# A random-feature attention and a feed-forward block on one core: queue orders, engines and buffer places written anew, and warming matmuls that read the identity

## The chip, the cores and the metric

One NeuronCore of a Trainium2 chip runs the whole kernel. The metric is the device time of one execution in microseconds (us), and the figure of a kernel is the median over its runs. TensorE is PE below (its weight loads PEld), VectorE is DVE, ScalarE is ACT, GpSimd is POOL, and SyncE, whose queue issues the kernel's DMAs, is SP.

## What is computed

```python
# q, k, v: 8 batches x 8 heads x 576 tokens x 64; omega: 128 x 64; w_in: 512 x 2048; w_out: 2048 x 512
def phi(x):                                   # x is q or k, times 64 ** -0.25
    h = einsum('bhsd,md->bhsm', x, omega) - sum(x * x, -1, keepdims=True) / 2
    return exp(h - max(h, -1, keepdims=True)) / sqrt(128)
kv  = einsum('bhsm,bhsd->bhmd', phi(k), v);  z = sum(phi(k), axis=2)
num = einsum('bhsm,bhmd->bhsd', phi(q), kv)
den = einsum('bhsm,bhm->bhs', phi(q), z)[..., None] + 1e-06
x   = (num / den) laid out as 4608 tokens x 512
h   = x @ w_in
out = maximum(0.01 * h, h) @ w_out            # 4608 x 512, float32
```

The weights come as 64-bit words, and the kernel makes them into floats itself.

## The kernel before

The 4608 tokens are done in nine blocks of 512. For block j the kernel needs the keys of the batches that the block touches (`key_batch`), the queries of the block (`query_block`) and the two layers of the feed-forward part (`feed_forward`). Almost every float32 product is made of three float16 matmuls: a number is split into a high part (`high`, a copy into float16 on ACT or DVE) and a low part (`low_`, a subtraction on POOL or DVE, line 699), and high by high, high by low and low by high are summed in PSUM.

Keys and queries go, a pair of heads at a time, through these steps. A DMA brings the rows (`nat`), ACT squares them (L936), DVE sums the squares (L938) and makes a power of two as a scale (L943 to L950), the rows are split (`z`) and turned by a DMA transpose (`t`), PE projects them on omega into the bank `pj` (L976), DVE takes the maxima (L984) and the scaled difference (L1004), ACT the exponentials, and the result is split into `ph`. The first batch of keys, the second one and the first block of queries (`Whole`) use float32 matmuls instead and need no transpose (L1060, L1076, L1078). Values by keys are summed in a bank `mi` (L1189 or L1201 to L1203) and split into `kv` (L1223). The numerators of the queries are products of `qp` and `kv` into a bank `mi` (L1313 in block 0, L1306 to L1308 after it); DVE takes the reciprocal of the denominators (L1324, L1328) and multiplies (L1330), which writes `xp` and frees the bank.

While the first keys and queries are done, the 16 pieces of the two weight matrices are loaded, put together from their words (L825 to L855, on ACT, DVE and POOL), measured (L845, L733 to L742) and split (L693, L691, L896). The first layer of blocks 0 and 1 is L1468, the second layer L1704. From block 2 on the first layer uses seven products in place of eight (L1522), and the last block does so in both layers (L1629).

There is no scheduler at run time. Each engine has a queue, and a queue runs in the order in which its instructions were written. The functions above do not emit instructions: they record operations (`Plan.op`) with the engines on which each may run, what it reads and writes, and the buffers it uses. A planner (`Plan.forward`) gives each operation an engine, each buffer one of the places of its kind (two `nat` tiles, three `ph` tiles, two `mi` banks and so on), and fills idle time of PE at the beginning with matmuls whose result nobody reads (`heat`, L783). After it, `Plan.order` puts the operations into the order of the table `ORDER`, with the engines of the table `ON`. An operation waits for the last users of a buffer's place, so an order and the places together set who waits for whom.

```python
            done = [by[n] for n in ORDER]
        nc.tensor.matmul(tiles["mi"][1][:, 4 * E:4 * E + 240], om[:, 0, :],
                         om.rearrange("p a b -> p (a b)")[:, :240], start=True, stop=True)
```

The second of these is the warming matmul: it needs `om`, the split omega, which DVE makes from `omT` with a power of two (L733 to L742, L771 to L776). `ident` is the identity, a DMA of its own (L754), which the matmul at L733 reads to spread a maximum over the partitions.

Of the kernel before, what the change touches and what calls it, by code (L numbers as in the profile page):

```python
# [17 lines left out]
P = 128  # L18
# [23 lines left out]
PASSES = 0  # L42
SHIFT_OP = {180: -1.13, 6: -3.99, 178: 2.07, 213: -0.22, 420: 3.05, 572: -0.02, 480: -0.72, 242: -1.74, 250: -2.72, 106: -1.06, 268: -4.94, 148: -4.28, 85: -4.22, 813: 0.8, 510: 2.03, 109: 2.11, 452: 11.66, 574: 2.34, 243: -2.55, 245: -6.52, 430: 4.22, 69: 19.05, 135: 1.83, 476: -3.51, 209: -10.73, 167: 1.07, 75: -11.31, 536: -3.21, 54: 2.69, 203: -3.67, 218: -23.73, 152: 1.07, 137: -0.51, 238: -0.14, 168: 2.42, 811: 24.59, 116: -2.3, 454: -3.25, 518: -0.29, 44: 0.47, 494: -5.44, 239: -5.28, 580: 6.23, 191: -6.7, 855: 8.61, 275: -6.71, 236: 4.8}
# [35 lines left out]

class Buf:  # L80
# [211 lines left out]
class Plan:  # L292
# [70 lines left out]
    def backward(self, done):  # L363
# [3 lines left out]
        for o in done:  # L367
            o.needs = {x.number: x for x in o.before}
            for b in o.bufs:
# [4 lines left out]
                for x in (x for u in at_[b] for x in u.ops):  # L374
                    o.needs[x.number] = x
# [1435 lines left out]
```

## Time and profile before

| what | value |
|---|---|
| runs | 907.95, 909.09 and 909.64 us; median 909.09 us |
| the profiled execution, first to last instruction (its span) | 907.4 us |
| what the median has around that span | 1.7 us |
| PE busy | 887.9 us, 98% of the span |
| DVE busy | 790.7 us, 87% |
| ACT busy | 536.3 us, 59% |
| POOL busy | 240.5 us, 27% |

The profile gives the span of the profiled execution and no other time of it, so its own time is taken as the median's 909.1 us: the span and 1.7 us around it. A share of busy time is a mean over stages. The stages are: the first 100 us, with weights, keys and queries in float32; up to 165 us, the first layer of block 0 and the beginning of its second layer, with the keys of batch 2 and the queries of block 1; then a long stretch of feed-forward work; and the last block's end from 890 us. In the windows below, each engine's busy time stands with the number of its instructions behind it, then the granted share of PE's clock, the busy share of the 16 DMA engines and their GB/s.

### The profile page before, as it was taken

The numbers are of one execution on the slowest core, as the hardware profiler recorded it, in microseconds if no ns is written. First come the engines' busy times: TensorE is split into PE (matmuls) and PEld (weight loads), VectorE is DVE, ScalarE is ACT, GpSimd is POOL, SyncE is SP. The second block draws the span as 40 slices with busy tenths as digits, with TensorE's granted clock in tenths as the row PEclk, the third lists the DMA queues.
The fourth block names the chain that finished last, engine by engine and source line by source line (L and its number), as shares of the span: only waits on it lengthen the run. The fifth ranks groups of instructions, "written<-read, shape, count | busy, mean of one in ns | idle before, by whom it ended". The sixth has DMA issues, their size and how long they took to land.

```text
span 907.4 us, 20572 instructions
## 1 busy us (share of the span) xinstructions
PE 887.9 (98%) x8257; PEld 640.6 (71%) x8257; DVE 790.7 (87%) x1571; ACT 536.3 (59%) x825; POOL 240.5 (27%) x236
## 2 busy tenths in 40 slices
PE   7999989999999999999999999999999999999998
PEld 6888545554556975688568855886579656888887
DVE  7999989978999999999998999899998999952771
ACT  5688877467655774477546854686557533522530
POOL 2332234456341330220211330132001101331340
PEclk9999999999999999999999999999999999999999
DMA  9757456766899979897899897987999636443401
GB/s 353 282 212 220 123 122 139 181 179 138 180 225 230 270 209 208 231 251 178 195 231 225 196 257 167 245 232 157 187 201 252 156 78 215 146 101 115 164 1 47
DMA packets 274879, 170.13 MB, mean 187 GB/s; under 512 B 191072, under 2 KB 237920, under 8 KB 273760
## 3 DMA queue, kind: packets, MB, share of 16 engines
q1 hardware_dynamic: 274784, 168.82, 73.3%
q8 instruction: 64, 1.05, 0.5%
q14 instruction: 31, 0.25, 0.1%
HBM read 105.87 MB, written 16.78 MB: 135 GB/s over the span
## 4 chain that ended last, share of the span: by engine, by line
PE 75%; DVE 12%; DMA 6%; ACT 4%; issue 2%; SPq 1%; POOL 0%; ACTq 0%; DVEq 0%
PE late L1522 14%; PE late L1704 13%; PE ffn L1704 13%; PE ffn L1522 13%; PE pj L976 5%; PE late L1629 5%; PE ffn L1629 3%; PE late L1468 2%; PE ffn L1468 2%; DMA t<-qT 1%; PE mi L1306 1%; DMA nat<-kT 1%; DVE wt L835 1%; PE mi L1308 1%; PE mi L1307 1%
## 5 line engine op out<-in xcount | busy, mean ns | idle before, releaser
L1522 PEld LDWEIGHTS <-w 128*128 128x128 f16 x2352 | 228.0, 98 | 30.4 <-issue 0.5
L1704 PEld LDWEIGHTS <-big 128*128 128x128 f16 x1344 | 127.7, 98 | 138.2
L699 POOL TENSOR_TENSOR big<-row,big 128x512 f16<-128x512 f32 x76 | 92.5, 1222 | 307.1 <-ACT big L693 189.8
L1704 PE MATMUL late<-wt,big 128*128 128x512 f16 x672 | 157.5, 379 | 0.0
L1704 PE MATMUL ffn<-wt,big 128*128 128x512 f16 x672 | 157.0, 379 | 0.0
L1522 PE MATMUL late<-xt,w 128*128 128x256 f16 x864 | 117.9, 273 | 0.0
L1522 PE MATMUL ffn<-xt,w 128*128 128x256 f16 x840 | 114.9, 273 | 0.4 <-DMA xt<-v 0.4
L1007 ACT ACTIVATE p<-p,little 128x1024 f32<-128x1024 f32 (+1 forms) x60 | 61.0, 1016 | 63.0 <-DVE p L1004 52.9
L984 DVE TENSOR_REDUCE st<-pj 128x8 f32<-128x1024 f32 x68 | 73.2, 1077 | 10.6 <-PE pj L976 10.4
L699 DVE TENSOR_TENSOR ph<-p,ph 128x1024 f16<-128x1024 f32 x56 | 69.3, 1238 | 5.4 <-ACT ph L693 4.7
L1004 DVE SCALAR_TENSOR_TENSOR p<-pj,sc,st 128x1024 f32<-128x1024 f32 (+1 forms) x60 | 67.0, 1117 | 0.8
L1468 PEld LDWEIGHTS <-w 128*128 128x128 f16 x384 | 36.6, 98 | 40.3
L693 ACT ACTIVATE big<-row 128x512 f16<-128x512 f32 x92 | 56.3, 622 | 8.5 <-DVE row L1494 7.7
L1545 ACT ACTIVATE row<-row 128x512 f32<-128x512 f32 x71 | 43.7, 625 | 26.6 <-DVE row L1538 25.6
L936 ACT ACTIVATE z<-nat 128x512 f32<-128x512 f32 (+1 forms) x56 | 36.2, 646 | 31.8 <-DMA nat<-qn 16.2
L1522 PE MATMUL late<-w,w 128*128 128x256 f16 x324 | 53.0, 273 | 0.0
L1522 PE MATMUL ffn<-w,w 128*128 128x256 f16 x324 | 53.0, 273 | 0.0
L1468 PE MATMUL ffn<-xt,w 128*128 128x512 f16 x216 | 50.9, 379 | 0.0
L693 ACT ACTIVATE ph<-p 128x1024 f16<-128x1024 f32 x47 | 49.6, 1055 | 0.9
L699 POOL TENSOR_TENSOR v<-xp,v 128x1024 f16<-128x1024 f32 (+1 forms) x10 | 20.5, 2055 | 109.0 <-DVE v L689 49.4
L852 POOL TENSOR_TENSOR wt<-wt,wt 128x1024 f32<-128x1024 f32 x10 | 25.4, 2550 | 69.8 <-ACT wt L850 36.4
L938 DVE TENSOR_REDUCE sq<-z 128x8 f32<-128x512 f32 (+1 forms) x56 | 39.4, 705 | 4.1 <-ACT z L936 3.9
(300 smaller groups left out, 1893.3 us busy)
## 6 DMA issues: line engine op xcount, KB each, us to landing
w<-w1d SPq DMA_DIRECT2D x196, 256.0 KB, 3.8
v<-vn SPq DMA_DIRECT2D x28, 650.0 KB, 5.0
big<-w_in SPq DMA_DIRECT2D x8, 1024.0 KB, 10.3
big<-w_out SPq DMA_DIRECT2D x8, 1024.0 KB, 5.7
nat<-qn SPq DMA_DIRECT2D x32, 256.0 KB, 3.4
out<-row SPq DMA_DIRECT2D x31, 256.0 KB, 3.0
w1d<-wt SPq DMA_DIRECT2D x16, 256.0 KB, 3.4
nat<-kn SPq DMA_DIRECT2D x12, 320.0 KB, 4.7
```

What stands on the lines that cost most here:

```text
L693: ("ACT", act(n, int(pointer)), lambda: nc.scalar.activation(dst(), src(), AF.Copy, scale=1.0 if scale is None else value()), False),
L699: return ways([(e, c, lambda g=g: g.tensor_tensor(dst(), a(), b(), op=ALU.subtract), True) for e, c, g in (("POOL", pool_(n), nc.gpsimd), ...
L938: op("DVE", dve(n), lambda: nc.vector.tensor_reduce(at(self.sq)[:, :2 * nt], square().rearrange("p (g d) -> p g d", d=D), axis=AX.X, op=AL ...
L976: nc.tensor.matmul(at(pj)[:, 512 * h + c * M:512 * h + (c + 1) * M], at(self.t)[:, 2 * (c0 + c) + h, :], om[:, w, :], start=(w == 0), stop ...
L984: op("DVE", dve(n * M), lambda: nc.vector.tensor_reduce(row(0), pv(), axis=AX.X, op=ALU.max), r=[pj], w=[st], prio=prio)
L1004: op("DVE", dve(n * M), lambda: nc.vector.scalar_tensor_tensor(p(), pv(), down(), row(2).rearrange("p (g o) -> p g o", o=1).broadcast_to([ ...
L1007: op("ACT", act(n * M, 1), lambda: nc.scalar.activation(flat(p()), flat(p()), AF.Exp, bias=shift), w=[p32], r=["ones"], prio=prio)
L1468: nc.tensor.matmul(at(ph), wk[wp][:, c:c + P], xt[:, 512 * xp:512 * xp + 512], start=(i == 0), stop=(i == 3 * KT - 1))
L1522: nc.tensor.matmul(pair(bank)[:, f], wt[:, k, wp, f * P:f * P + P], operand(xname, k, xp), start=(first and f == k == i == 0), stop=(k == ...
L1545: op("ACT", act(512), lambda: nc.scalar.activation(at(g), at(src), AF.Prelu, scale=H_DOWN * (TAIL_DOWN if tail else 1.0), alpha=0.01), r=[ ...
L1629: nc.tensor.matmul(pair(bank)[:, t], g()[:, gp, f, t * P:t * P + P], operand(wname, 2 * q + f, wp), start=(first and q == t == f == i == 0 ...
L1704: nc.tensor.matmul(at(po), g_(q)[:, s, gp, t * P:(t + 1) * P], wf[wp], start=(q == s == 0 and gp == wp), stop=(q == s == 3 and gp == 1))
```

## The change

The planner's passes go (`backward`, `PASSES`, `SHIFT_OP`). Where there is an `ORDER`, `forward` is no longer run: the order, each operation's engine (`ON`, or the first engine that the operation allows) and now also each buffer's place (`PLACES`) come from tables, which are all new. Negative numbers in `ORDER` are warming matmuls, so many as the number says. The warming matmul reads `ident` instead of `om`, and so waits for that DMA alone.

```diff
+PLACES = {
+    "xt": [0, 1, 2, 3, 0, 1, 2, 3, 0, 5, 4, 1, 3, 2, 0, 1, 5, 3, 4, 1, 2, 0, 5, 1, 3, 2, 4, 0, 1, 3, 5, 2, 0],
...
 ORDER = [
-    2, 16, 1, 0, 27, 62, 144, 151, 17, 7, 3, 43, 9, 4, 28, 165, 18, 5, 6, 146, 145, 22, 19, 152, 3478, 81, 3461, 20,
...
     def order(self):
-        done = self.forward()
-        for _ in range(PASSES):
...
+        if not ORDER:
+            return self.forward()
+        for o in self.ops:
+            o.engine, o.heat = ON.get(o.number, next(iter(o.ways))), False
+            o.cost, o.run, o.held = o.ways[o.engine]
+        done, heaters = [], len(self.ops)
+        for n in ORDER:
+            if n >= 0:
+                done.append(self.ops[n])
+                continue
+            x = Op()
+            x.number, x.engine, x.heat, x.filler, x.held = heaters, "PE", True, True, False
+            x.cost, x.run = -0.1 * n, lambda n=n: self.warm[1](-n)
+            x.ways, x.before, x.bufs = {"PE": (x.cost, x.run, False)}, [self.warm[0]], []
...
+        self.settle(done)
         return done
+    def settle(self, done):
...
+                if b.place is None:
+                    b.place = PLACES[b.kind][nth[b]]
...
-                nc.tensor.matmul(tiles["mi"][1][:, 4 * E:4 * E + 240], om[:, 0, :],
-                                 om.rearrange("p a b -> p (a b)")[:, :240], start=True, stop=True)
-        plan.warm = done, heat
+                nc.tensor.matmul(tiles["mi"][1][:, 4 * E:4 * E + 240], ident.bitcast(F16)[:, :P],
+                                 ident.bitcast(F16)[:, :240], start=True, stop=True)
+        plan.warm = turner, heat
```

The operations are the same ones, and so is the number of matmuls that compute something. There are 106 warming matmuls where there were 137. Of the 3430 operations 264 have another engine: 100 copies of `high` go from ACT to DVE and 96 from DVE to ACT, 43 subtractions of `low_` (L699) go from DVE to POOL and 23 from POOL to DVE, and 4 scalings of the last block (L1649, L1653) trade ACT and DVE. In the first 100 us one operation alone has another engine; there the order is what changes. Lines of the changed kernel are 48 higher than those of the kernel before from `omega` on.

The first place is SP's queue at the start. `nat`, `xn` and `t` hold keys and queries (`kT`, `qT`), `big` a piece of `w_in`, `v` the values. Before:

```order
L1033 DMA nat_83<-kT 128x640
L754 DMA ident<-eye 128x128
L753 DMA xt_108<-omT 128x256
L1033 DMA nat_84<-kT 128x640
L1033 DMA xn_107<-qT 128x512
L810 DMA big_79<-w_in 128x2048
```

and in the change:

```order
L1081 DMA nat_83<-kT 128x640
L801 DMA xt_108<-omT 128x256
L858 DMA big_79<-w_in 128x2048
L1081 DMA xn_107<-qT 128x512
L1081 DMA nat_84<-kT 128x640
L802 DMA ident<-eye 128x128
```

Omega comes second instead of third, and the identity sixth instead of second, behind a piece of the weights of 1 MB. On PE the matmul that spreads omega's maximum (L733), the first one before, comes behind the projections of the first head pair, and the first ten warming matmuls come behind it.

The second place is SP's queue where the keys of batch 2 begin, at about 100 us. `nat<-kn` are the rows of a pair of heads, `t<-z` the transposes of queries of block 1. Before:

```order
L1108 DMA v_0_99<-vn 128x1300
L1381 DMA w1d<-w_7_68 128x4x256
L963 DMA_TRANSPOSE t_87<-z_85 128x8x128
L933 DMA nat_83<-kn 128x5x128
L963 DMA_TRANSPOSE t_87<-z_86 128x8x128
```

and in the change:

```order
L1156 DMA v_0_99<-vn 128x1300 x2
L981 DMA nat_83<-kn 128x5x128
L1011 DMA_TRANSPOSE t_87<-z_86 128x8x128
L1322 DMA_TRANSPOSE qp_96<-ph_89 128x8x128
```

The keys' rows stood behind the transpose of the third pair of queries and now stand ahead of it.

The third place is DVE's queue ahead of the first multiplications by a reciprocal of block 1. L1223 (L1271 in the change) writes `kv` of batch 0, L896 (L944) splits a piece of `w_out`, L1324 and L1330 (L1372, L1378) are the reciprocal's first step and the multiplication that frees a bank `mi`. Before:

```order
L1223 SCALAR_TENSOR_TENSOR kv_100<-mi_137,kv_100 128x4
L699 TENSOR_TENSOR big_80<-row_104,big_80 128x512
L1223 SCALAR_TENSOR_TENSOR kv_100<-mi_136,kv_100 128x4
L896 SCALAR_TENSOR_TENSOR wt_69<-wt_70,little,wt_69 128x1024
L1324 TENSOR_SCALAR r_124<-mi_137 128x4
```

and in the change:

```order
L1271 SCALAR_TENSOR_TENSOR kv_100<-mi_137,kv_100 128x4
L747 TENSOR_TENSOR z_85<-nat_84,z_85 128x8x64
L1042 SCALAR_TENSOR_TENSOR st_114<-st_114,sc_122,sq_118 128x8
L1043 SCALAR_TENSOR_TENSOR st_114<-sq_118,st_114 128x8
L1187 SCALAR_TENSOR_TENSOR v_98<-v_0_99,little,v_98 128x1280
L1052 SCALAR_TENSOR_TENSOR p_0_88<-pj_129,sc_122,st_114 128x1024
L944 SCALAR_TENSOR_TENSOR wt_77<-wt_73,little,wt_77 128x1024
L747 TENSOR_TENSOR z_86<-nat_83,z_86 128x10x64
L1372 TENSOR_SCALAR r_124<-mi_136 128x4
```

More of DVE's work on the weights, the keys and the values stands between `kv` and the multiplications. On PE, 66 matmuls of the second layer (L1704) now stand ahead of the fourth group of numerators of block 1, where before 6 did.

## Rows read from the trace of the kernel before

**Rows 1.** The page: each engine's busy time, share and instructions.

```profile
PE 887.9 (98%) x8257; PEld 640.6 (71%) x8257; DVE 790.7 (87%) x1571; ACT 536.3 (59%) x825; POOL 240.5 (27%) x236
```

**Rows 2.** Windows: us, busy time of PE, PEld, DVE, ACT, POOL; clock, DMA.

```profile
0.00:9.66 9.66, 4.05 (x38) 3.83 (x40) 3.62 (x18) 2.75 (x3) 0.20 (x4) 1.00 0.78 265
9.66:100.00 90.34, 85.71 (x962) 74.77 (x959) 86.50 (x130) 71.34 (x97) 25.05 (x11) 1.00 0.68 251
100.00:140.50 40.50, 37.27 (x248) 19.08 (x247) 36.41 (x87) 32.09 (x54) 13.95 (x20) 1.00 0.51 112
...
165.00:890.00 725.00, 723.04 (x6720) 519.03 (x6719) 636.59 (x1289) 414.00 (x652) 189.37 (x184) 1.00 0.77 186
```

**Rows 3.** The warming matmuls of L783 alone: busy time of PE and PEld.

```profile
9.66:100.00 90.34, 15.73 (x137) 12.80 (x137) 1.00 0.68 251
```

**Rows 4.** The chain that ended last, 100 to 170 us: start, us, engine, tile.

```profile
114.07 6.19 DMA nat<-kn
...
141.66 5.18 PE late L1704 x24
```

**Rows 5.** The timeline, 100 to 142 us: start, us, instruction, [idle before, releaser].

```profile
112.76 1.25 SPq L963 DMA_TRANSPOSE t<-z  x1
...
121.10 0.82 DVE L938 TENSOR_REDUCE sq<-z 128x10 f32<-128x640 f32 x1 [2.66 <-ACT z L936]
...
129.44 2.75 PE L1468 MATMUL late<-xt,w 128*128 128x512 f16 x12
...
140.52 0.19 PE L1306 MATMUL mi<-kv,qp 128*128 128x65 f16 x1
```

**Rows 6.** DVE's groups over the whole span: busy us, mean ns of one.

```profile
L699 DVE TENSOR_TENSOR ph<-p,ph 128x1024 f16<-128x1024 f32 x56 | 69.3, 1238 | 5.4 <-ACT ph L693 4.7 <-DMA qp<-ph 0.3
L984 DVE TENSOR_REDUCE st<-pj 128x8 f32<-128x1024 f32 x56 | 68.2, 1218 | 7.4 <-PE pj L976 7.3
L699 DVE TENSOR_TENSOR big<-row,big 128x512 f16<-128x512 f32 x49 | 34.6, 712 | 1.1 <-ACT big L693 1.0
L1139 DVE SCALAR_TENSOR_TENSOR v<-v,little,v 128x1280 f16<-128x1280 f32 x12 | 19.8, 1650 | 0.0
L896 DVE SCALAR_TENSOR_TENSOR w<-wt,little,w 128x1024 f16<-128x1024 f32 x6 | 7.7, 1278 | 0.0
L699 DVE TENSOR_TENSOR z<-nat,z 128x512 f16<-128x512 f32 x12 | 8.2, 684 | 0.7 <-ACT z L693 0.7
```

**Rows 7.** PE's groups in the stretch from 100 to 165 us: busy us, mean ns.

```profile
L1468 PE MATMUL late<-xt,w 128*128 128x512 f16 x58 | 13.8, 379 | 0.0
L976 PE MATMUL pj<-om,t 128*128 128x128 f16 x64 | 4.2, 219 | 1.5 <-ACT p L1001 1.4
```

**Rows 8.** The timeline of the first 10 us.

```profile
1.66 0.42 SPq L753 DMA_DIRECT2D xt<-omT  x1
...
4.81 0.29 DVE L765 TENSOR_SCALAR xt<-xt 128x256 f32<-128x256 f32 x1 [3.14 <-DMA xt<-omT]
...
8.20 0.64 PE L1060 MATMUL pj<-xt,nat 64*128 64x128 f32 x4
...
9.00 0.39 PE L1060 MATMUL pj<-xt,nat 64*128 64x128 f32 x4
...
9.66 1.23 DVE L1076 TENSOR_REDUCE st<-pj 128x8 f32<-128x1024 f32 x1 [0.79 <-PE pj L1060]
```

**Rows 9.** DVE's copies of L689 (min/median/max ns), and one beside a subtraction on POOL.

```profile
L689 DVE CAST big<-row x33: 414/418/1376, 105.2 to 870.8; 128x512 f16<-128x512 f32 x33
...
212.30 1.40 POOL L699 TENSOR_TENSOR big<-row,big 128x512 f16<-128x512 f32 x1
212.61 1.38 DVE L689 CAST big<-row 128x512 f16<-128x512 f32 x1
```

**Rows 10.** PE's longest wait for a DMA behind 165 us, in the timeline.

```profile
489.07 0.20 PE L1308 MATMUL mi<-kv,qp 128*128 128x65 f16 x1 [0.65 <-DMA qp<-ph]
```

**Rows 11.** One window of 50 us, the columns as in rows 2.

```profile
250.00:300.00 50.00, 48.69 (x457) 31.22 (x455) 48.86 (x95) 31.92 (x45) 15.43 (x14) 1.00 0.99 235
```

More of the change, by code (lines that the diff above doesn't have):

```diff
@@ L77 @@
 PRICE = {"PE": 1.0, "ACT": 0, "DVE": 27.4627, "POOL": 1.0804, "SP": 1.0}
+PLACES = {
[3 rows of a table added]
+    "raw": [0, 1, 3, 2, 0, 1, 3, 0, 2, 1, 3, 2],
+    "sqz": [0, 1, 0, 2, 1, 0, 2, 0, 1, 2, 1, 0],
[8 rows of a table added]
+    "edge": [0, 1, 2, 3, 0, 1, 2, 3, 0, 1, 2, 3, 0, 1, 2, 3],
[6 rows of a table added]
+    "ffn": [0, 1, 0, 0, 1, 1, 1, 0, 1, 1, 0, 1, 0, 1, 3, 0, 2, 1, 1, 0, 3, 2, 3, 0, 1, 2, 3, 1, 0, 2, 3, 1, 0, 0, 3,
[7 rows of a table added]
+    "big": [1, 0, 0, 2, 3, 1, 2, 3, 0, 1, 3, 0, 2, 2, 1, 3, 0, 2, 1, 3, 0, 2, 1, 3, 0, 2, 1, 3, 0, 2, 1, 3, 0, 2, 1,
[4 rows of a table added]
+    "row": [0, 1, 0, 2, 3, 1, 0, 1, 2, 3, 1, 0, 3, 2, 1, 0, 2, 3, 1, 2, 0, 3, 1, 2, 1, 3, 0, 2, 3, 1, 0, 2, 3, 1, 0,
[6 rows of a table added]
+    "nat": [0, 1, 0, 1, 0, 0, 1, 0, 1, 0, 1, 0, 1, 0, 1, 0, 1, 0, 1, 0, 1, 0, 1, 0, 1, 0, 1, 0, 1, 0, 1, 0, 1, 0, 1,
[13 rows of a table added]
+    "ring": [4, 1, 2, 9, 6, 3, 4, 0, 8, 5, 1, 3, 7, 2, 9, 0, 4, 6, 5, 8, 9, 3, 7, 2, 1, 0, 8, 4, 9, 4, 7, 3, 5, 6, 2,
[8 rows of a table added]
+}
 class Buf:
@@ new lines @@
+    700: "DVE", 705: "DVE", 725: "DVE", 734: "DVE", 770: "DVE", 790: "DVE", 854: "DVE", 914: "DVE", 923: "DVE",
+    953: "DVE", 1008: "DVE", 1011: "DVE", 1015: "DVE", 1024: "DVE", 1033: "DVE", 1036: "DVE", 1046: "DVE",
+    1053: "DVE", 1061: "DVE", 1084: "DVE", 1096: "DVE", 1100: "DVE", 1110: "DVE", 1116: "DVE", 1117: "DVE",
+    1140: "DVE", 1160: "DVE", 1170: "DVE", 1180: "DVE", 1218: "DVE", 1289: "DVE", 1304: "DVE", 1345: "DVE",
+    1399: "DVE", 1404: "DVE", 1410: "DVE", 1411: "DVE", 1423: "DVE", 1430: "DVE", 1431: "DVE", 1442: "DVE",
@@ new lines @@
+    1454: "DVE", 1469: "DVE", 1474: "DVE", 1486: "DVE", 1492: "DVE", 1560: "DVE", 1597: "DVE", 1636: "DVE",
+    1688: "DVE", 1695: "DVE", 1755: "DVE", 1772: "DVE", 1824: "DVE", 1837: "DVE", 1844: "DVE", 1845: "DVE",
+    1874: "DVE", 1879: "DVE", 1957: "DVE", 2004: "DVE", 2034: "DVE", 2052: "DVE", 2066: "DVE", 2102: "DVE",
+    2104: "DVE", 2123: "DVE", 2147: "DVE", 2162: "DVE", 2172: "DVE", 2190: "DVE", 2210: "DVE", 2219: "DVE",
+    2254: "DVE", 2264: "DVE", 2304: "DVE", 2326: "DVE", 2342: "DVE", 2372: "DVE", 2384: "DVE", 2387: "DVE",
@@ new lines @@
+    2402: "DVE", 2448: "DVE", 2483: "DVE", 2484: "DVE", 2497: "DVE", 2509: "DVE", 2512: "DVE", 2523: "DVE",
+    2532: "DVE", 2540: "DVE", 2549: "DVE", 2554: "DVE", 2555: "DVE", 2573: "DVE", 2580: "DVE", 2581: "DVE",
+    2587: "DVE", 2592: "DVE", 2615: "DVE", 2626: "DVE", 2667: "DVE", 2678: "DVE", 2693: "DVE", 2718: "DVE",
+    2740: "DVE", 2752: "DVE", 2762: "DVE", 2777: "DVE", 2794: "DVE", 2853: "DVE", 2855: "DVE", 2857: "DVE",
+    2873: "DVE", 2885: "DVE", 2901: "DVE", 2903: "DVE", 2905: "DVE", 2923: "DVE", 2926: "DVE", 2941: "DVE",
@@ L285 @@
+    2953: "DVE", 2965: "DVE", 2980: "DVE", 2995: "DVE", 3019: "DVE", 3022: "DVE", 3025: "DVE", 3080: "DVE",
+    3150: "DVE", 3166: "DVE", 3180: "DVE", 3195: "DVE", 3218: "DVE", 3219: "DVE", 3228: "DVE", 3232: "DVE",
+    3240: "DVE", 3252: "DVE", 3255: "DVE", 3261: "DVE", 3270: "DVE", 3274: "DVE", 3294: "DVE", 3297: "DVE",
+    3316: "DVE", 3324: "DVE", 3339: "DVE", 3354: "DVE", 3363: "DVE", 3387: "DVE", 3403: "DVE",
 }
@@ L345, in order @@
     def order(self):
-        done = self.forward()
-        for _ in range(PASSES):
-            late = self.backward(done)
-            for o in self.ops:
-                if not o.filler and o.prio > -0.9:
-                    o.prio = -0.5 + 1e-4 * (late[o.number] + SHIFT_OP.get(o.number, 0.0))
-            done = self.forward()
-        if ORDER:
-            by = {o.number: o for o in done}
-            assert len(by) == len(ORDER)
-            for n, e in ON.items():
-                o = by[n]
-                o.engine, (o.cost, o.run, o.held) = e, o.ways[e]
-            done = [by[n] for n in ORDER]
@@ L361, in order @@
-        return done
-    def backward(self, done):
-        held, at_ = {}, {}
-        done = [o for o in done if not o.heat]
+        if not ORDER:
[12 more added lines that the diff above has]
+            x.ways, x.before, x.bufs = {"PE": (x.cost, x.run, False)}, [self.warm[0]], []
+            heaters += 1
+            done.append(x)
@@ new lines, in order @@
+        assert sorted(o.number for o in done if not o.heat) == list(range(len(self.ops)))
+        self.settle(done)
+        return done
+    def settle(self, done):
+        shared = {}
+        for k, hosts in self.over.items():
+            for h in hosts:
+                shared.setdefault(k, []).append(h)
+                shared.setdefault(h, []).append(k)
+        user, last, nth = {}, {}, {b: i for bs in self.kinds.values() for i, b in enumerate(bs)}
+        for bs in self.kinds.values():
+            for b in bs:
+                b.place, b.left = None, len(b.ops)
@@ L367, in backward @@
         for o in done:
-            o.needs = {x.number: x for x in o.before}
             for b in o.bufs:
-                if b not in at_:
-                    hosts = [(b.kind, b.place), *self.over.get((b.kind, b.place), ())]
-                    at_[b] = [held[k] for k in hosts if k in held]
-                    held[b.kind, b.place] = b
-                for x in (x for u in at_[b] for x in u.ops):
-                    o.needs[x.number] = x
-            o.needs.pop(o.number, None)
-        left = dict.fromkeys((o.number for o in done), 0)
@@ L378, in backward @@
-        for o in done:
-            for x in o.needs:
-                left[x] += 1
-        last = max(o.end for o in done)
-        until, late = dict.fromkeys(left, last), {}
-        free = dict.fromkeys(("PE", "ACT", "DVE", "POOL", "SP"), last)
-        port = last
-        todo = [o for o in done if not left[o.number]]
-        while todo:
-            cost = lambda o: o.cost - self.LESS[o.engine]
-            def latest(o):
-                r = min(until[o.number] - (o.end - o.start - cost(o)), free[o.engine])
-                return min(r, port) if o.held else r
-            o = max(todo, key=lambda o: (latest(o), o.start))
-            start = latest(o) - cost(o)
-            todo.remove(o)
-            late[o.number] = free[o.engine] = start
-            if o.held:
-                port = start
-            for n, x in o.needs.items():
-                until[n] = min(until[n], start)
-                left[n] -= 1
-                if not left[n]:
-                    todo.append(x)
@@ L403, in backward @@
-        return late
+                if b.place is None:
+                    b.place = PLACES[b.kind][nth[b]]
+                    assert b.place < self.places[b.kind]
+                    hosts = [(b.kind, b.place), *shared.get((b.kind, b.place), ())]
+                    assert not any(user.get(k) for k in hosts), f"{b.kind} {nth[b]} has a place in use"
+                    user[b.kind, b.place] = b
+                b.left -= 1
+                if not b.left:
+                    user[b.kind, b.place] = None
@@ L777, in split @@
                                                op1=ALU.subtract)
-        done = op("DVE", 1.3, split, r=[(whole, "om"), key], w=["om", "om_c"], prio=0.005)
+        op("DVE", 1.3, split, r=[(whole, "om"), key], w=["om", "om_c"], prio=0.005)
         def heat(n):
             for _ in range(n):
-                nc.tensor.matmul(tiles["mi"][1][:, 4 * E:4 * E + 240], om[:, 0, :],
-                                 om.rearrange("p a b -> p (a b)")[:, :240], start=True, stop=True)
-        plan.warm = done, heat
+                nc.tensor.matmul(tiles["mi"][1][:, 4 * E:4 * E + 240], ident.bitcast(F16)[:, :P],
+                                 ident.bitcast(F16)[:, :240], start=True, stop=True)
+        plan.warm = turner, heat
     class Weight:
```

29 lines of the change are left out of this document (3 added, 26 removed), and 397 rows, old and new, of tables (ORDER, PLACES).

## Prediction

> **What bounds the kernel now.** I read the page first, then windows, then the chain of waits, then the timeline. The page says PE 98% [rows 1], which invites the conclusion that only PE's work counts. The windows correct it [rows 2]. From 165 to 890 us PE is without work for 725.00 - 723.04 = 2.0 us. In the 9.66 us of the start it idles 5.6; up to 100 us it idles 90.34 - 85.71 = 4.6, and 15.7 of its busy time is warming [rows 3], so 20.4 us go without arithmetic that counts; from 100 to 140.5 us it idles 3.2. Some 29 of its 31 lost microseconds lie ahead of 140.5 us. The engine that is full there is DVE: 86.50 of 90.34 and 36.41 of 40.50 us. The chain of waits agrees [rows 4]: ahead of 140 us it runs over DVE and a load of keys, and from 141.66 us it stays on PE. So there are two regimes. Up to about 140 us DVE sets the pace; after it, PE executes a fixed amount of work without holes. **The end comes earlier by as much as PE has more work done when the last long wait for DVE ends.** That wait's end is the fourth group of numerators of block 1, which started at 140.52 us [rows 5]: it needs a bank `mi` that DVE frees at L1330 (L1378). I count what each queue has ahead of that one operation, before and after, from the orders and the durations in the rows.
>
> **PE's queue.** In the change 66 matmuls of L1704 stand ahead of these numerators where 6 did, so 60 are newly done by then (of the 66 newly ahead, 6 replace six of L1468). Twelve such matmuls in one run take 2.75 us [rows 5] and one alone 0.379 [rows 7], so one follows another at (2.75 - 0.379) / 11 = 0.2155 us: 12.9 us. Sixteen projections of L976 come ahead as well, at 4.2 / 64 = 0.066 [rows 7]: 1.05. Eighteen numerators, 65 columns wide against the projections' 128, at half of that: 0.6. Sum 14.6 us of PE work that no longer stands behind the wait.
>
> **DVE's queue.** Newly ahead of the bank's release [rows 6]: three splits of L896 at 1.278, two of L1139 at 1.650, a maximum of L984 at 1.218, a scaled difference of L1004 that I price by the like 128x1024 form of L896 at 1.278, a `ph` subtraction at 1.238, two `z` subtractions at 0.684. Together 12.2. Seven short ones have no row of their own; at the 0.29 of a 128x256 instruction [rows 8] they are 2.0. No longer ahead: four subtractions of `big` at 0.712 (2.85) [rows 6], two copies of L689 and four conversions of L691, all at a copy's 0.418 [rows 9] (2.5). Net +8.8 us. If DVE idles as before, the wait ends 8.8 us later and has 14.6 us more PE work behind it: **-5.8 us.** The bounds of the small terms (numerators from nothing to 1.2 us, the seven from 1 to 4) move this by about 2 us either way.
>
> **DVE's idle time, in the middle.** The largest hole of DVE between 100 and 140.5 us is 2.66 us ahead of L938 [rows 5]: it waits for ACT's squares, and these for the keys' rows, a load that is issued behind a transpose of 1.25 us on SP at 112.76 and takes 6.19 us [rows 4, 5]. In the change that load stands ahead of the transpose (the second place), so its start no longer hangs on when that transpose can start. I take the hole to close: -2.7. Its ends are 0, if `nat`'s place frees no earlier, and -4.1, all of the idle time of that window [rows 2]. What is late next there is the third transpose; projections stand behind it, and DVE has other work queued meanwhile.
>
> **DVE's idle time, at the start.** Omega's load moves up one issue of about 0.45 us, and the projections no longer wait for L733. DVE's first reduction of them, now at 9.66 us [rows 8], can come at about 8.6: omega landed by 4.81 - 0.45, 0.75 us for L765 and L766, then eight quads at the slow spacing of 0.43 us (3.4), as the quads of 0.64 us show the array at half pace until about 8.9 us, against 0.39 after it [rows 8]. That gains 1.0 us on the clock but moves ten of the 18 instructions that DVE did in those 9.66 us behind the reduction (L737 to L742, L771 to L776): 3.62 x 10 / 18 = 2.0 us [rows 2]. Net +1.0, between 0 and +2. The identity, sixth behind 1 MB of weights, lands later than before, but nothing except L733 and the warming reads it.
>
> **Warming.** 31 fewer at 15.73 / 137 = 0.115 us [rows 3] are 3.6 us less on PE in a stretch where PE waits for DVE; I cost that at nothing. Where PE would be late instead, it gives up to that back. The granted clock is 1.00 from 9.66 us on [rows 2].
>
> **Engines.** 264 operations trade engines, one of them before 100 us, so this is a matter of the long stretch. There DVE has 725 - 637 = 88 us of idle time [rows 2] and PE is the bound; I cost it at nothing. What it costs if that cover goes is the third rival.
>
> **Sum:** -5.8 - 2.7 + 1.0 = -7.5 us. The profiled execution takes 907.4 us and 1.7 around it, 909.1 in all, which is the median of the runs (907.95 to 909.64): **901.6 us.**
>
> **A rule against the change.** A `big` copy of DVE takes 0.418 us as a rule, and 1.38 where it started 0.3 us behind a subtraction on POOL of 1.40 us: both ended together [rows 9]. The change gives POOL 43 subtractions of DVE and takes 23 away. Taken as free of each other, the exchange relieves DVE by 20 x 0.712 = 14 us [rows 6]; if each of the 20 met one copy like that, DVE would lose 20 x (1.376 - 0.418) = 19 us [rows 9], and the 88 us of idle time would still cover it. The Trainium skill, page "SBUF — State Buffer", section "SBUF: two separate sides", says that VectorE and GpSimd share one pair of ports as an exclusive lock: who starts first holds it for its whole instruction. The trace agrees, with 1.38 against 0.418. By that rule a subtraction given to POOL may cost DVE time instead of saving it.
>
> **Rivals.**
> *First, everything goes (0.15).* The order closes the other holes as well: DVE's 3.84 us of idle time from 9.66 to 100 us, and the 1.4 left of the window after it [rows 2]. 901.6 - 5.2 = 896.4. For it: the whole order is new, not those two places. Against it: part of these holes is the wait for weights, whose bytes are the same.
> *Second, PE earns it and pays it back (0.14).* PE that is 7.5 us ahead meets loads that are not. From 250 to 300 us the DMA engines are busy 0.99 of the time and PE already loses 1.3 us [rows 11]; at 489 us it waits 0.65 for a transpose [rows 10]. If the stretch is really at DMA's pace, the gain shrinks to nothing: 909. Against it: over the whole stretch the DMA share is 0.77 [rows 2], and DVE's work is due less late in the new order.
> *Third, a copy that waits for POOL (0.09), slower.* A copy that falls behind a POOL subtraction is late by 1.376 - 0.418 = 0.96 us [rows 9]. If PE has to wait for what such a copy leads to, the gain is used up at 7.5 / 0.96, eight times; at ten of the 43 it is 909.1 + 9.6 - 7.5 = 911.2. Against it: the 88 us of slack on DVE, and PE's waits for DVE behind 165 us are within the 2.0 us of now.
> *Fourth, the start does not do what it says (0.07).* With the identity late and fewer warming matmuls PE may fall back to half pace after a gap. Up to 100 us it has 85.7 - 15.7 = 70 us of work that counts [rows 2, 3]; if 6 us of it ran at half pace, DVE would wait up to 6 us more, and I take half of that: 904.6. Against it: of 137 warming matmuls 106 stay.
>
> **Chances.** The forecast, 899 to 905, has 0.55. The range 896.0 to 909.0 takes in the first and fourth rivals and what lies between the forecast and the second; left out are most of the second, and the third. A measurement of this kernel tells about 0.2% from no change, 1.8 us: faster (under 907.3) 0.77, the same 0.13, slower (over 910.9) 0.10.
>
> **What would show it.** Right: the numerators of block 1's fourth group at about 147.6 us (140.5 + 8.8 - 2.7 + 1.0), with PE without holes after them; L938 with no 2.66 us ahead of it; the first reduction at 8.6; 165 to 890 us with 2 us of PE idle or less. Wrong: more than 4 us of idle PE there, with DMA or POOL as releaser (second and third rivals); granted clock under 1.00 after 10 us (fourth); that group later than 150 us, which would say that DVE found new holes.

## The result, and the profile after

The changed kernel takes **897.62 us** (median of four runs, 896.87 to 898.18) against 908.52 us of the kernel before beside it: a ratio of 0.9878, interval 0.9865 to 0.9891, so 10.9 us less. The forecast was 901.6 us, 7.5 less, in a range from 896.0 to 909.0. The result lies in the range but below the 899 to 905 that had the largest chance, and nearer to the first rival's 896.4 than to the forecast. The profiled execution took 896.87 us, with a span of 894.9; the span of before was 907.4, so the two traces differ by 12.5 us, 1.6 more than the medians. What follows is an account of the traces.

The windows of the changed kernel, with the columns of [rows 2] (us, busy time of PE, PEld, DVE, ACT, POOL; granted clock, DMA):

```profile
0.00:9.66 9.66, 4.56 (x40) 4.35 (x40) 2.78 (x9) 2.82 (x3) 0.20 (x4) 1.00 0.78 278
9.66:100.00 90.34, 89.03 (x968) 75.00 (x969) 88.14 (x147) 77.23 (x108) 29.59 (x19) 1.00 0.69 247
100.00:140.50 40.50, 40.50 (x274) 20.86 (x273) 39.60 (x81) 36.59 (x56) 18.26 (x18) 1.00 0.59 129
140.50:165.00 24.50, 23.89 (x188) 12.03 (x187) 23.68 (x47) 12.54 (x18) 16.78 (x19) 1.00 0.90 214
165.00:880.00 715.00, 713.98 (x6665) 515.09 (x6665) 620.50 (x1268) 397.15 (x634) 214.42 (x198) 1.00 0.77 187
```

PE idles 1.3 us from 9.66 to 100 us, where it idled 4.6 [rows 2], nothing from 100 to 140.5 (3.2 before), 0.6 in the window after it, and 1.0 from 165 to 880. DVE's holes shrink as well: 2.2 us up to 100 us (3.84 before), 0.9 up to 140.5 (4.1 before). The page gives each engine's sum; [rows 1] is the same row before:

```profile
PE 882.9 (99%) x8226; PEld 636.9 (71%) x8226; DVE 778.1 (87%) x1555; ACT 527.9 (59%) x821; POOL 279.2 (31%) x256
```

DVE works 12.6 us less than before and POOL 38.7 us more. The share of DVE, 87%, is the same in both; a mean over the whole span hides what the experiments below bring out. The timeline at the places of which the prediction spoke (start, us, instruction, [idle before, releaser]; [rows 5, 8] are their counterparts):

```profile
1.20 0.42 SPq L801 DMA_DIRECT2D xt<-omT  x1
...
3.08 0.43 SPq L802 DMA_DIRECT2D ident<-eye  x1
...
8.28 1.56 DVE L1124 TENSOR_REDUCE st<-pj 128x8 f32<-128x1024 f32 x2 [3.43 <-PE pj L1108]
...
10.65 0.46 PE L781 MATMUL mi<-ident,little 128*128 128x128 f32 x2 [1.64 <-DMA ident<-eye]
...
10.95 1.19 PE L831 MATMUL mi<-ident 128*128 128x240 f16 x10
...
14.18 1.22 DVE L1124 TENSOR_REDUCE st<-pj 128x8 f32<-128x1024 f32 x1
...
109.94 0.38 SPq L981 DMA_DIRECT2D nat<-kn  x1
...
119.85 0.78 ACT L984 ACTIVATE z<-nat 128x640 f32<-128x640 f32 x1
...
122.08 0.81 DVE L986 TENSOR_REDUCE sq<-z 128x10 f32<-128x640 f32 x1
...
141.81 1.46 PE L1516 MATMUL ffn<-xt,w 128*128 128x512 f16 x6
...
142.69 0.41 DVE L1378 TENSOR_TENSOR xp<-mi,r 128x256 f32<-128x256 f32 x1
...
143.15 0.19 PE L1354 MATMUL mi<-kv,qp 128*128 128x65 f16 x1
```

The first reduction comes at 8.28 us (forecast 8.6). The reduction of the keys' squares (L986) has no idle time ahead of it where there were 2.66 us. The fourth group of numerators of block 1 starts at 143.15, a twentieth of a microsecond behind the end of the multiplication (142.69 + 0.41) that frees its bank. PE has no idle time ahead of it: six matmuls of L1516 from 141.81 on, one every 0.2155 us, end their turn at 143.1 as well. DVE and PE reach the group together, and this trace alone does not say which of them sets its start; the first two experiments do. The forecast for it was 147.6.

From that group to the end of the span there were 907.4 - 140.52 = 766.9 us and there are 894.9 - 143.15 = 751.75: **15.1 us less**, of which the prediction had 14.6. Of the 15.1, 14.7 are PE's work (760.8 us of busy time behind the group before, 746.1 now) and the rest is idle time. The group itself came 2.6 us later, where the prediction had 7.1. (The text on the change says that 66 matmuls of L1704 now stand ahead of the group; there are 72, of which 66 are new. With the six of L1468 that are gone, the net 60 of the sum is right.)

### The profile page after: what moved, and what is told of

Same layout as the page of the kernel before. It is cut to its first block, busy times and chain, and to the rows that moved or that the text cites. A ratio compares the mean times of both kernels' runs of the same rounds, so it can differ in the third digit from the quotient of the medians.

```text
span 894.9 us, 20507 instructions
## 1 busy us (share of the span) xinstructions
PE 882.9 (99%) x8226; PEld 636.9 (71%) x8226; DVE 778.1 (87%) x1555; ACT 527.9 (59%) x821; POOL 279.2 (31%) x256
## 4 chain that ended last, share of the span: by engine, by line
PE 85%; DVE 9%; ACT 2%; DMA 2%; issue 1%; SPq 0%; DVEq 0%; ACTq 0%
PE late L1570 15%; PE ffn L1752 14%; PE late L1752 13%; PE ffn L1570 12%; PE ffn L1677 5%; PE pj L1024 5%; PE ffn L1516 4%; PE late L1516 3%; PE late L1677 3%; PE pj L1108 2%; PE mi L1237 2%; DVE ph L747 1%; DVE p L1052 1%; PE mi L831 1%; DVE st L1032 1%
## 5 line engine op out<-in xcount | busy, mean ns | idle before, releaser
L1752 PEld LDWEIGHTS <-big 128*128 128x128 f16 x1344 | 128.2, 98 | 138.5 <-issue 0.7
L747 POOL TENSOR_TENSOR big<-row,big 128x512 f16<-128x512 f32 x85 | 110.8, 1311 | 309.5 <-ACT big L741 220.4
L1752 PE MATMUL ffn<-wt,big 128*128 128x512 f16 x672 | 157.1, 379 | 0.6 <-ACT row L1525 0.6
L1752 PE MATMUL late<-wt,big 128*128 128x512 f16 x672 | 157.5, 379 | 0.0
L1570 PE MATMUL late<-xt,w 128*128 128x256 f16 x942 | 127.8, 273 | 0.0
L1570 PE MATMUL ffn<-xt,w 128*128 128x256 f16 x762 | 104.4, 273 | 0.0
L1516 PEld LDWEIGHTS <-w 128*128 128x128 f16 x384 | 36.2, 98 | 39.3 <-issue 0.4
L1570 PE MATMUL late<-w,w 128*128 128x256 f16 x342 | 56.0, 273 | 0.0
L1570 PE MATMUL ffn<-w,w 128*128 128x256 f16 x306 | 50.1, 273 | 0.0
L1516 PE MATMUL ffn<-xt,w 128*128 128x512 f16 x204 | 48.6, 379 | 0.1
L741 ACT ACTIVATE ph<-p 128x1024 f16<-128x1024 f32 x41 | 43.1, 1051 | 0.5
L1516 PE MATMUL late<-xt,w 128*128 128x512 f16 x180 | 42.6, 379 | 0.0
L747 POOL TENSOR_TENSOR v<-xp,v 128x1024 f16<-128x1024 f32 (+2 forms) x12 | 22.9, 1905 | 60.8 <-ACT v L741 60.8
```

The source lines that it names most:

```text
L741: ("ACT", act(n, int(pointer)), lambda: nc.scalar.activation(dst(), src(), AF.Copy, scale=1.0 if scale is None else value()), False),
L747: return ways([(e, c, lambda g=g: g.tensor_tensor(dst(), a(), b(), op=ALU.subtract), True) for e, c, g in (("POOL", pool_(n), nc.gpsimd), ...
L1516: nc.tensor.matmul(at(ph), wk[wp][:, c:c + P], xt[:, 512 * xp:512 * xp + 512], start=(i == 0), stop=(i == 3 * KT - 1))
L1570: nc.tensor.matmul(pair(bank)[:, f], wt[:, k, wp, f * P:f * P + P], operand(xname, k, xp), start=(first and f == k == i == 0), stop=(k == ...
L1752: nc.tensor.matmul(at(po), g_(q)[:, s, gp, t * P:(t + 1) * P], wf[wp], start=(q == s == 0 and gp == wp), stop=(q == s == 3 and gp == 1))
```

## The experiments

Theory A was the prediction's: DVE's queue up to 143 us sets the pace, PE's work ahead of that wait is what is earned, and what lies behind it is PE's alone. Each kernel was timed beside the kernel before; the kernels are the changed one with its tables edited, except where another base is named. "Against the change" is the difference of a kernel's ratio to 0.9878, at 0.1% to 0.9 us.

**PE's work back behind the wait.** The 11 operations of L1752, six matmuls each, that are new ahead of the group (505) go behind it:

```diff
 ORDER = [
-    ... 378, ... 387, ... 388, ... 379, ... 397, ... 398, ... 389, ... 399, ... 400, ... 401, ... 380, ... 505,
+    ... 505, 378, 387, 388, 379, 397, 398, 389, 399, 400, 401, 380,
```

> The change with the 66 matmuls of the second layer (L1752) that it brought ahead of that group of numerators put behind it again, 11 runs of 6; DVE's queue is untouched. Theory A (DVE's queue sets when the group starts, and PE work ahead of it is what the change earns): the group still starts at about 143 us, PE idles in the place of 66 x 0.2155 = 14.2 us, and the end comes up to 14.2 us later: 909 to 912. Rival C (since 73 us PE is without a hole in the changed kernel, so PE alone bounds it, and the group would come earlier if less stood ahead of it): 898 to 901, the group at 129 to 133 us.

Measured: 912.29 us beside 908.65, ratio 1.0039 (1.0025 to 1.0054): 14.6 us against the change. The timeline of PE (the last wait of 5.81 us is for a multiplication on DVE):

```profile
129.03 0.19 PE L1330 MATMUL mi<-kv,qp 128*128 128x65 f16 x1 [3.80 <-DVE kv L1247]
...
132.84 1.89 PE L1000 MATMUL pj<-om,t 128*128 128x128 f16 x16 [2.22 <-DMA t<-z]
...
140.54 0.27 PE L1330 MATMUL mi<-kv,qp 128*64 128x65 f16 x2 [5.81 <-DVE xp L1354]
...
143.89 0.26 PE L1330 MATMUL mi<-kv,qp 128*128 128x65 f16 x1
```

With 14.2 us of work less ahead of it the group still starts at 143.89, and PE stands idle for 11.8 us in three waits, two on DVE. DVE's multiplication ends at 143.08 here and at 143.10 in the change; the last 0.8 us are PE's own, six matmuls in 2.55 us, where the granted clock is 0.51 from 129.0 to 143.9 us. From the group to the end there are 910.5 - 143.89 = 766.6 us, 14.9 more than in the change. Theory A's term is shown, and rival C, by which the group would have come at about 130 us, is out. The granted clock was 0.84 in the window from 100 to 143 us in which PE idled, part of the price.

**DVE's queue made longer, at two places.** Two maxima whose result nobody reads (2.4 us), ahead of the multiplication (479) at 142.7 us, or ahead of an operation at 300 us:

```diff
+            nc.vector.tensor_reduce(spare, ident.rearrange("p (o n) -> p o n", o=1).broadcast_to([P, 8, P]),
+                                    axis=AX.X, op=ALU.max)
```

> The change with two maxima over 1024 elements, whose result nobody reads, added on DVE ahead of the reciprocal's multiplication (L1378) that frees the bank for the fourth group of numerators of block 1 (142.7 us): about 2.4 us. Theory A (DVE's queue ahead of that group sets the end, and there is no slack): +2.0 to +2.6, 899.6 to 900.2. Rival C (PE alone bounds the changed kernel from 73 us on): 0 to +0.5.

> The same two maxima added on DVE at 300 us. Theory A (behind 165 us PE is the bound and DVE has slack): 0 to +0.5, 897.5 to 898.1. Rival G (DVE is as full there and the long stretch is tight too): +2.0 to +2.6.

Measured: early 901.52 us, ratio 0.9925 (0.9912 to 0.9937), 4.3 us against the change; late 899.08 us, ratio 0.9902 (0.9888 to 0.9915), 2.2 us. The timelines of PE, of the early one:

```profile
148.84 0.19 PE L1336 MATMUL mi<-kv,qp 128*128 128x65 f16 x1 [2.26 <-DVE xp L1360]
```

and of the late one:

```profile
303.53 1.47 PE L1552 MATMUL ffn<-xt,w 128*128 128x256 f16 x12 [1.89 <-DVE row L1568]
```

The early result is theory A's and more than its range: PE waits 2.26 us at the group, so there was no slack between the two engines. In the profiled execution (the slowest of its six) the group is 5.7 us late: 2.4 are the maxima, and 3.3 were lost at the start (last section); the clock is at 0.96 from 140 to 180 us. Why the median of the six lost 4.3 and not 2.4 is not shown, as the other five have no trace. The late result refutes theory A's other half. At 300 us DVE's idle time does not cover it: 2.4 us more on DVE make PE wait 1.89 us a few microseconds later, where the change has no wait. Rival G was right.

**The load of keys.** In the kernel before, the load ahead of the transpose; in the change, behind it:

```diff
-    332, 474, 518, 270, 337, 808, 495,
+    332, 474, 808, 518, 270, 337, 495,
```

```diff
-    274, 808, 272, 474, 518, 275,
+    274, 272, 474, 518, 808, 275,
```

> The kernel before with one DMA moved on SP's queue: the load of batch 2's keys stands ahead of the third transpose of block 1's queries instead of behind it. The prediction's term: the 2.66 us that DVE idles ahead of L938 (L986 here) go, and the end comes 2.7 us earlier: 905 to 906.5. Rival F (the load and the transpose wait for the same subtraction, which reads the rows in the place the load wants and writes what the transpose reads, so only the transpose's issue of 1.25 us is saved, and the hole in the change closed because DVE had other work queued there): the hole shrinks to about 1.4 us, 907 to 908.5.

> The change with the load of batch 2's keys put behind that transpose again. The prediction's term: +2.7 us, 900.3. Rival F: DVE's queue has 2.2 us of other work between the rows' arrival and L986, so +0 to +0.5: 897.5 to 898.2.

Measured: load first, 909.02 us beside 908.56, ratio 1.0006 (0.9997 to 1.0015); load behind, 899.11 us, ratio 0.9890 (0.9875 to 0.9905), 1.1 us against the change, and each ratio lies within the other's interval. The timeline of the kernel before with the load first:

```profile
111.95 0.37 SPq L959 DMA_DIRECT2D nat<-kn  x1
112.44 1.72 SPq L989 DMA_TRANSPOSE t<-z  x1
...
119.04 0.82 DVE L964 TENSOR_REDUCE sq<-z 128x10 f32<-128x640 f32 x1 [1.79 <-ACT z L962]
```

The hole went from 2.66 to 1.79 us, and the time did not follow. Load and transpose start 0.5 us apart behind the end of the same subtraction (`z`, 110.81 to 111.49 us). In the change with the load behind, L962 (the reduction) starts at 123.60 with no idle time ahead of it: DVE's new order has other work there. Its group of numerators came at 144.67, 1.5 us late, and as much was lost at the start already (DVE's second reduction at 15.68 us in place of 14.18). The place in SP's queue was not what closed the hole.

**The subtractions back.** All 66 trades between DVE and POOL undone, the order as in the change (an operation not in the table runs on POOL):

```diff
 ON = {
-    360: "DVE", 484: "DVE", 620: "DVE", 668: "DVE", 680: "DVE",
+    315: "DVE", 320: "DVE", 340: "DVE", 350: "DVE", 365: "DVE",
...
```

> The change with the 43 subtractions back on DVE and the 23 back on POOL; order and all else as in the change. Theory A (the long stretch has idle time on DVE, so the trade costs nothing): 896.5 to 899. Rival D (POOL's subtractions hold up DVE's copies at the shared port, so fewer of them help): 893 to 896. Rival E (20 subtractions of 0.71 us more on DVE, 14 us, reach PE): 900 to 910.

Measured: 914.95 us beside 908.65, ratio 1.0074 (1.0053 to 1.0095): **17.8 us** against the change, and slower than before. Two of PE's waits, from its timeline:

```profile
109.77 0.35 PE L872 MATMUL mi<-ones,wt 128*128 128x1 bf16 x8 [1.00 <-DVE wt L862]
...
118.73 0.49 PE L760 MATMUL mi<-ident,little 128*128 128x128 f32 x2 [3.10 <-DVE little L764]
```

and its windows (PE busy is the first number behind the width):

```profile
100.00:140.50 40.50, 36.32 (x210) 17.95 (x208) 39.38 (x74) 32.02 (x51) 10.64 (x7) 0.96 0.45 98
...
165.00:890.00 725.00, 717.02 (x6650) 513.00 (x6649) 643.32 (x1297) 402.18 (x641) 195.20 (x185) 1.00 0.76 186
```

Net, 20 subtractions of 0.71 us are 14 us on DVE. Four of the trades lie ahead of 140.5 us, all four from DVE to POOL, so DVE has 2.8 us more there; PE idles 4.2 us in the first window, where the change had none. In the second, with 58 of the trades, it idles 8.0 us; the change had 1.0. The group of numerators comes at 149.42, 6.3 us late, and from it to the end there are 9.8 us more than in the change. Rival E, not theory A. Rival D, by which POOL's port costs DVE more than its work saves, is refuted for this order: what POOL's subtractions take off DVE outweighs what they hold up. The 17.8 us are more than the 14 of DVE's work, and the order and the places are still the ones that go with the trades; how much of the price is theirs was not tried.

**The change's order ahead of a cut, the order of before behind it.** Order, engines and places are the change's up to the group at 143 us, or up to 300 us. A first pair joined one kernel's half ahead of the group with the other's half behind it. It came out at 909.46 us (ratio 1.0005) with the change's half first and at 912.94 (1.0047) with the old half first; but some buffers ahead of the cut had the other kernel's places, so that neither half was the original, and the pair settles nothing by itself.

> The change's order, engines and places up to the fourth group of numerators of block 1 (143 us in the changed kernel), the order and engines of the kernel before behind it; two operations of the next load of keys come a little later. Theory A (the gain is made ahead of that group, where DVE set the pace): nearly all of the 10.9 us stays; behind 140 us PE idles 2.0 us in the kernel before and 1.6 in the changed one, so 898 to 899. Rival B (the gain comes from the engines and the order of the long stretch, the shared port among them): most of it goes, 904 to 908.

> The converse: the order and engines of the kernel before up to the same group of numerators (140.5 us there), with its warming on omega, and the change's behind it. Theory A: 907 to 909, about the kernel before. Rival B: 899 to 903.

The repetition has the change's places up to the cut. Behind it stand the remaining operations in the order of before, with its engines and, where free, places; at the cut of 143 us:

```diff
 ORDER = [
...
     577, 527, 548, 505,
-    578, 372, 831, 294, 549, 572, 390, 1183,
+    570, 564, 563, 573, 359, 360, 372, 370,
...
```

> head_new again, with the places of the change for every buffer that is first used ahead of the cut, so that the part ahead of it is the change's to the last operation; behind the cut (143 us) the order, the engines and, where free, the places of the kernel before. Theory A (all is earned ahead of the cut): 897.5 to 899. Theory I (PE runs 15 us further ahead of the rest at the cut, and the order and engines behind it have to keep DVE up with it, or the gain is given back in new waits for DVE): 902 to 910, with PE idle between 150 and 180 us.

> The same with the cut at 300 us: 202 of the 264 trades of engines, 45 of the 66 with POOL among them, are undone, all behind the cut. Theory A: 897.5 to 899. Theory I in the strong form (DVE is all but full up to 700 us, so the trades are needed all along): 901 to 908, PE's new waits spread over 300 to 700 us. In the weak form (only the 40 us behind the cut at 143 us had been tight): 897.5 to 900.

Measured: cut at 143 us, 909.34 us beside 908.83, ratio 1.0012 (0.9998 to 1.0025): everything is given back. Cut at 300 us: 904.98 us, ratio 0.9962 (0.9947 to 0.9977), 3.5 us faster than before and 7.6 behind the change. PE's waits, cut at 143 us:

```profile
145.16 2.75 PE L1729 MATMUL ffn<-wt,big 128*128 128x512 f16 x12 [0.75 <-ACT row L1502]
154.66 0.39 PE L1729 MATMUL ffn<-wt,big 128*128 128x512 f16 x1 [1.43 <-DVE big L724]
169.63 0.59 PE L1001 MATMUL pj<-om,t 128*128 128x128 f16 x4 [3.79 <-DVE p L1029]
171.16 2.72 PE L1493 MATMUL late<-xt,w 128*128 128x512 f16 x6 [0.95 <-ACT row L718]
```

and cut at 300 us:

```profile
309.43 1.47 PE L1548 MATMUL ffn<-xt,w 128*128 128x256 f16 x12 [3.45 <-DVE row L1564]
```

Behind either cut PE runs into work of DVE or ACT that is not done. In the first case it idles 6.9 us from 143 to 180 us and has a granted clock of 0.91 there. DVE is not full in that stretch: it works 26.75 of 37 us (35.22 in the change) and waits itself, longest for the squares of a pair of keys. In the change these squares start at about the same time (151.85 us in place of 152.42), but DVE has other work ahead of them, and its reduction follows at 156.17 without a wait. DVE's wait with the old order, and the window (DVE is the third sum behind the width):

```profile
153.19 0.82 DVE L963 TENSOR_REDUCE sq<-z 128x10 f32<-128x640 f32 x1 [6.69 <-ACT z L961]
...
143.00:180.00 37.00, 30.09 (x210) 14.86 (x207) 26.75 (x64) 14.17 (x20) 17.05 (x23) 0.91 0.73 172
```

So just behind 143 us it is the old order that fails, and not too much work on DVE. At 300 us it is otherwise: from 300 to 320 us DVE works 19.03 of 20 us, and PE idles 3.9. Theory I holds for the size, but not in its strong form: from 320 to 700 us, with all the trades there undone, PE idles 0.6 us. The profiled execution of this kernel had also lost 1.9 us ahead of the cut, at the start (the group at 145.07). How much of the waits a new order of the old tail could avoid was not tried.

**The start.** The identity's DMA third in place of sixth:

```diff
-    2, 16, 0, 151, 43, 27, 1, 17,
+    2, 16, 0, 1, 151, 43, 27, 17,
```

> The change with the identity's DMA third on SP's queue, right behind omega's, in place of sixth behind a 1 MB piece of the weights. Theory H (PE stands 1.6 to 2.4 us in wait of the identity at 8.7 us, with the second pair's projections behind it, and in some runs falls back to half pace there, which puts DVE's second reduction at 17.5 in place of 14.2 us): the wait goes, the runs lie closer together, 894.5 to 897. Rival J (DVE has 0.2 us of idle time behind its first reduction and is what bounds, so the wait costs nothing): 897 to 898.5.

Measured: 897.18 us, ratio 0.9878 (0.9864 to 0.9893): no difference. PE's wait of 1.64 us is gone, and the time is as it was; DVE, which had 0.17 us of idle time behind its first reduction, was the bound there, so rival J is right for the median. The three runs counted took 896.82 to 897.51 us; the fourth took 2375.98 and is left out.

**No warming at all.** Every negative number is taken out of the order:

> The change without any warming matmul (106 in all, 10.9 us of PE). The prediction's cost of nothing for 31 fewer: PE waits for DVE in that stretch, so the time that they take is free, and the clock alone can suffer. If the clock holds: 897 to 898.5. If PE falls to half pace in its gaps ahead of 73 us (the prediction's fourth rival): 900 to 908, with a granted clock under 1.00 in windows of the first 73 us.

Measured: 897.81 us, ratio 0.9895 (0.9875 to 0.9915), 1.5 us against the change and with the change's 0.9878 inside the interval. Five of the six runs took 896.96 to 898.53. The sixth, the profiled one, took 903.24 and shows a granted clock of 0.90 from 50 to 100 us:

```profile
50.00:100.00 50.00, 48.11 (x422) 39.10 (x419) 44.98 (x75) 41.74 (x59) 15.46 (x12) 0.90 0.49 166
```

In that run the group of numerators came at 149.43, 6.3 us late, and behind it nothing was lost. So the 106 warming matmuls, 12.7 us of PE's busy time in the change, take no time away and give the median none; what they may buy is that a run like the sixth is rarer, which six runs cannot show.

## Why the prediction was right, point by point, and where its reasons were not

**PE's queue, -14.6: right.** PE's work behind the group fell by 14.7 us in the traces. Putting the 66 matmuls back added 14.9 us behind the group, for 14.2 of work.

**The place of the last wait: not quite.** The prediction took the group at 140.52 us for the end of a wait for DVE. In the trace of the kernel before, PE had no idle time ahead of it:

```profile
138.29 0.19 PE L1307 MATMUL mi<-kv,qp 128*128 128x65 f16 x1 [0.26 <-DVE kv L1223]
...
139.23 1.46 PE L1704 MATMUL late<-wt,big 128*128 128x512 f16 x6
...
139.88 0.73 DVE L1330 TENSOR_TENSOR xp<-mi,r 128x256 f32<-128x256 f32 x2
```

The first of the two multiplications ended at 140.27, before PE's six matmuls let it reach the group at 140.52. The last wait for DVE was the 0.26 us at 138.29. As PE has no hole between the two, the sum does not change.

**DVE's queue, +8.8, and its idle time, -2.7 and +1.0: the terms that were mis-sized.** They make 7.1 us, and the group came 2.6 later. The windows split the gap of 4.5. DVE's idle time up to the group was 14.0 us and is 9.66 - 2.78 = 6.9, 2.2 and 0.9, so 10.0: 4.0 less in place of 1.7 less. The hole from 9.66 to 100 us, from which the forecast took nothing, gave 1.6 of it. That and the 0.5 by which the middle gave more than its 2.66 are the first rival, two fifths of its 5.2 come true. The start's +1.0 was about right, at 0.8. The other 2.2 us are DVE's work: 6.6 us more busy time in place of 8.8. The instructions were priced well: summed by their durations, those ahead of the group come to 138.0 us before and 146.6 in the change, 8.6 more. But an instruction's duration can be longer than the step to the next, as DVE's timeline in the changed kernel shows:

```profile
131.38 1.28 DVE L1052 SCALAR_TENSOR_TENSOR p<-pj,sc,st 128x1024 f32<-128x1024 f32 x1
132.57 1.28 DVE L944 SCALAR_TENSOR_TENSOR wt<-wt,little,wt 128x1024 f16<-128x1024 f32 x1
133.76 0.82 DVE L747 TENSOR_TENSOR z<-nat,z 128x640 f16<-128x640 f32 x1
```

1.19 us from start to start, 1.28 long. For PE the prediction used spacings, for DVE durations. Over the whole queue up to the group such overlaps come to 11.4 us before and 13.5 in the change, and the difference of 2.1 is nearly the whole gap of 2.2.

**The load of keys: the hole closed, for another reason.** The prediction put -2.7 us on the load's place in SP's queue. The load waits for the same subtraction as the transpose, and moving it alone gave nothing. In the change, and with the load behind, DVE has other work up to the reduction; its own order closed the hole.

**Warming: right as far as tested.** Taking out all of it cost nothing in the median; the 31 fewer were not tried alone.

**Engines, nothing, covered by 88 us of idle time on DVE: wrong as a reason, and the largest error among the reasons.** At 300 us, 2.4 us more on DVE cost 2.2. Undoing a quarter of the trades costs 17.8 us, and undoing the 254 that lie behind 143 us, together with the order there, costs the whole gain. The 88 us were a sum over 725. In the kernel before, these windows show it (DVE's busy time is the third sum behind the width):

```profile
300.00:400.00 100.00, 100.00 (x993) 72.65 (x991) 94.17 (x202) 61.33 (x99) 22.66 (x18) 1.00 0.93 226
400.00:500.00 100.00, 99.35 (x1000) 72.18 (x999) 93.38 (x204) 62.07 (x95) 17.84 (x25) 1.00 0.88 215
800.00:890.00 90.00, 90.00 (x827) 80.66 (x825) 49.60 (x81) 30.64 (x57) 24.95 (x20) 1.00 0.32 94
```

Of the 88 us, 40 lie behind 800 us. From 300 to 500 us DVE is at 93 to 94%. A PE that is 15 us ahead needs a DVE whose work is done earlier as well. In the change it is: DVE's busy time behind the group is 645.0 us where it was 664.2, 19.2 less, of which 6.6 stand ahead of the group now and 12.6 are gone from the kernel (the trades with POOL, 20 subtractions net, are worth 14). The old order behind 143 us does not keep this up, with DVE itself waiting there. How the price divides between the trades, the order and the places stays open. This is the second rival's mechanism (PE runs into work that is not there), on DVE and not on the DMA queues, and the prediction gave it 0.14 on other grounds. In the change it did not come about: PE idles 1.0 us behind 165 us. The term came out near nothing because the work on DVE was taken away and put into another order, and not because DVE had slack; in that part the forecast was lucky.

**The third rival, POOL's port.** It stayed out, and with the order of the change the trade works the other way: fewer subtractions on POOL make the kernel slower. The copies of `big` on DVE do better than before [rows 9]:

```profile
L737 DVE CAST big<-row x32: 396/418/524, 111.5 to 849.4; 128x512 f16<-128x512 f32 x32
```

The longest is 0.524 us where it was 1.376. POOL has more work, and other instructions of DVE are longer than before: the `z` subtractions take 0.811 us on average where they took 0.684 [rows 6], by the same view of the changed kernel:

```profile
L747 DVE TENSOR_TENSOR z<-nat,z 128x512 f16<-128x512 f32 x12 | 9.7, 811 | 0.0
```

The four `z` subtractions that took over 0.9 us each started within 0.3 us behind the start of an instruction on POOL. The longest one stands beside a pair of subtractions of 1.16 us, the second of which started at 91.54:

```profile
90.42 2.28 POOL L747 TENSOR_TENSOR big<-row,big 128x512 f16<-128x512 f32 x2 [0.29 <-ACT big L741]
91.73 1.51 DVE L747 TENSOR_TENSOR z<-nat,z 128x512 f16<-128x512 f32 x1
```

The lock that the Trainium skill, page "SBUF — State Buffer", section "SBUF: two separate sides", describes is not contradicted by these rows; as far as they go, what counts is which instruction stands beside which, more than how many subtractions POOL has.

## What to carry to other kernels

Idle time cannot be lent from one stage to another: before an edit is priced at nothing because an engine has slack, read that engine's windows where the edit lands, and ask whether the engine would still be in time if the one it serves came earlier. Where two engines run level, a gain on one was kept here only where the other's queue behind it fitted, in its load and in its order; the forecast of a large reordering then needs a sum for each engine. And count work in a full queue by the steps from start to start, not by durations: here the overlaps alone took 2.1 us off a term of 8.8.

## What the runs showed of the hardware

The same start can run at different paces. In the changed kernel the matmul on the identity waits for its DMA until 10.65 us, takes 0.46 us, and the ten warming matmuls after it 1.19. In the kernel with the early maxima, whose order is the same up to 140 us, the timeline of the profiled execution shows:

```profile
11.20 0.76 PE L757 MATMUL mi<-ident,little 128*128 128x128 f32 x2 [2.15 <-DMA ident<-eye]
...
11.76 2.21 PE L813 MATMUL mi<-ident 128*128 128x240 f16 x10
...
17.46 1.22 DVE L1106 TENSOR_REDUCE st<-pj 128x8 f32<-128x1024 f32 x1 [2.97 <-PE pj L1090]
```

The wait for the identity was 2.15 us in place of 1.64, the same matmuls ran at about half the pace, and DVE's second reduction came at 17.46 us where the changed kernel has it at 14.18. Two more profiled executions with the same start had the second reduction late: 15.68 us with the load behind, and 16.07 with the cut at 300 us. The granted clock does not tell them apart from the others in every case. From 8 to 17 us it is 0.81 in these two, but 1.00 both in the changed kernel and with the early maxima, so that the pace of the first microseconds is better read from the matmuls' own times. With the identity third in the queue the wait is gone, and three runs lie within 0.7 us. Whether that makes late starts rarer is open; three runs are too few. What makes a start slow is open as well.
